# The sign step of a norm's means on GpSimd instead of VectorE

## The chip, the cores and the metric

The kernel runs on one core of a Trainium2 chip. A core has five engines that run side by side and wait for one another through semaphores: TensorE (PE in the profile, its weight loads PEld), VectorE (DVE), ScalarE (ACT), GpSimd (POOL) and SyncE (SP), which here issues the DMAs. The metric is the device time of one execution in microseconds; of several runs the median is given.

## The reference

One transformer block is computed on 2048 tokens of width 512, in bf16. Each half has a norm without weights, a modulation by rows that come from a conditioning vector, a mixer, and a gated residual.

```python
x = A_x
h = _layernorm(x, axis=-1) * (1 + ca) + sa
x = x + ga * _A_ref(h, A_wqkv, A_wo)        # 32 heads of 16, causal window of 256 keys
h = _layernorm(x, axis=-1) * (1 + cb) + sb
x = x + gb * _B_ref(h, B_w1, B_b1, B_w2, B_b2)

def _layernorm(x, axis=-1, eps=1e-05):
    m = jnp.mean(x, axis=axis, keepdims=True)
    v = jnp.var(x, axis=axis, keepdims=True)
    return (x - m) / jnp.sqrt(v + eps)
```

`_B_ref` norms its input once more and then mixes over tokens: `u = gelu(h^T w1 + b1)` with 1792 hidden features, and `y = u w2 + b2`. So there are three norms per token: n1 ahead of attention, n2 behind it, and n3 inside the token mixer.

## The kernel before

The 2048 tokens are 16 blocks of 128 (partitions are tokens). `xres[t]` holds block t of the residual stream. Four blocks make a group `tg`. The program has three stages.

1. A prologue up to about 13 us: masks, the modulation, n1 of the first four blocks, the first query and key projections.
2. The attention stage, 16 steps of 4 heads on 512 queries each (`s` = 4·tg + g8). ScalarE takes 152 exponentials of 128x1024 (L868). TensorE makes the scores for them, and between the scores does the projections, the products with V (L890), the output projection `Wo` (L606 or L610 by its shape), and the first half of the token mixer. VectorE empties PSUM, transposes, and does the statistics of the norms.
3. The tail from about 157 us: `Wo` and the norms of the last four blocks (12 to 15) run while TensorE does the second half of the first token-mixing product (matmuls out<-hb,w1b on L606), and then the second token-mixing product (L1451) with its output steps.

A norm that is laid through the class `Norm` is done for 1, 2 or 4 blocks together. It has these instructions, in this order:

- `stats`: per block a BATCH_NORM_STATS2 (L599) and a BATCH_NORM_AGGREGATE (L600) on VectorE, which leave mean and variance side by side in the tile `mv`.
- `prepare`: on VectorE `ve` = variance + epsilon (L571) and `neg` = −mean (L575). The profile calls their outputs n1ve, n1ng, n2ve, and so on by the norm.
- `rstd`: on GpSimd `r` = ve to the power −1/2 (L582) and `shift` = neg · r (L584, n2sh and so on).
- `apply`: per block one instruction r·x + shift, on ScalarE (L588), or on VectorE or GpSimd (L592).

Behind n2's apply come two row operations, a multiplication by bc_cb and an addition of bc_sb (L1273), then n3's statistics, and n3's apply writes `hb[tb]`, the operand of the first token-mixing product. The tiles of `prepare` and `rstd` come from the pool `small`, 4 buffers to a name.

Which engine does what is set per block in the table `BY`, whose entries for the last blocks are

```python
'p2.12': 'POOL', 'k2.12': 'POOL', 'm2.12': 'DVE', 'p3.12': 'ACT',
'p2.13': 'POOL', 'k2.13': 'DVE', 'm2.13': 'DVE', 'p3.13': 'POOL',
'p2.14': 'ACT', 'k2.14': 'DVE', 'm2.14': 'DVE', 'p3.14': 'POOL',
'p2.15': 'DVE', 'k2.15': 'DVE', 'm2.15': 'DVE', 'p3.15': 'DVE',
```

(p2 and p3 are the applies of n2 and n3, k2 and m2 the row operations). How many blocks share a norm is set by `JOINT`; the last four blocks have one norm each. In all `prepare` runs 20 times: 3 for n1, 8 for n2, 9 for n3. Twelve are in the attention stage and eight, one of n2 and one of n3 for each of the blocks 12 to 15, in the tail.

The order of the work is made by a small planner (`Order`): every step is a task with an engine, a cost, what it needs, and a rank; the planner plays the engines forward, and `emit` then writes the tasks in order of their planned starts. Every engine executes its own instructions in the order in which they were written. A whole `prepare` is one task (`e1.`, `e2.`, `e3.`) with the engine "DVE" and a cost of 0.13, and a whole `rstd` is one task on "POOL" (`q2.`, `q3.`, `r1.`); GpSimd tasks that were planned between the two stand between them on GpSimd.

On TensorE the second half of the first token-mixing product goes through the tokens block by block: eight matmuls on hb_12, then eight on hb_13, eight on hb_14, and six on hb_15 ahead of the next features. The first matmul of each block waits for the engine that writes that block's `hb`: for ScalarE (12), GpSimd (13 and 14) and VectorE (15).

Of the kernel before, what the change touches and what calls it, by code (L numbers as in the profile page):

```python
# [347 lines left out]
def kernel(  # L348
# [14 lines left out]
    nc = tc.nc  # L363
# [194 lines left out]
    class Norm:  # L558
# [9 lines left out]
        def prepare(self):  # L568
            n = self.n
            self.ve = small.tile([P, n], DT.float32, name=self.name + "ve")  # L570
            nc.vector.tensor_scalar(  # L571
                out=self.ve[:], in0=self.mv[:, :, 1], scalar1=EPS, scalar2=0.0, op0=ALU.add, op1=ALU.add
            )
            self.neg = small.tile([P, n], DT.float32, name=self.name + "ng")
            nc.vector.tensor_scalar(  # L575
                out=self.neg[:], in0=self.mv[:, :, 0], scalar1=-1.0, scalar2=0.0, op0=ALU.mult, op1=ALU.add
            )

# [923 lines left out]
```

## Time and profile before

| | |
|---|---|
| time of 3 runs | 243.13 us median, 242.91 to 243.34 |
| profiled execution | 242.64 us, of it a span of 240.9 us |
| PE busy | 234.5 us (97%) |
| DVE busy | 177.3 us (74%) |
| ACT busy | 162.1 us (67%) |
| POOL busy | 96.1 us (40%) |
| sign step on DVE (L575) | 20 instructions |

The span is the time between the first and the last instruction of the profiled execution. An engine's share is a mean over stages with different limits: ScalarE is full during attention and nearly idle in the tail, while GpSimd has its work in bursts. The lines "idle before" name what ended a wait. In the tables of instructions below, the first number is the start in us from the start of the span, the second the duration.

### The profile page before, as it was taken

The numbers are of one execution on the slowest core, as the hardware profiler recorded it, in microseconds if no ns is written. First come the engines' busy times: TensorE is split into PE (matmuls) and PEld (weight loads), VectorE is DVE, ScalarE is ACT, GpSimd is POOL, SyncE is SP. The second block draws the span as 40 slices with busy tenths as digits, with TensorE's granted clock in tenths as the row PEclk, the third lists the DMA queues.
The fourth block names the chain that finished last, engine by engine and source line by source line (L and its number), as shares of the span: only waits on it lengthen the run. The fifth ranks groups of instructions, "written<-read, shape, count | busy, mean of one in ns | idle before, by whom it ended". The sixth has DMA issues, their size and how long they took to land.

```text
span 240.9 us, 9884 instructions
## 1 busy us (share of the span) xinstructions
PE 234.5 (97%) x4358; PEld 118.7 (49%) x4358; DVE 177.3 (74%) x421; ACT 162.1 (67%) x188; POOL 96.1 (40%) x149
## 2 busy tenths in 40 slices
PE   7999999999999999999999999999999999999994
PEld 2545555545655554554454455454444444444443
DVE  8799998878999899999356867989964306060644
ACT  7589999999999999999999999900446400000000
POOL 5319775741655466996310113686920000000000
PEclk9999999999999999999999999999999999999999
DMA  5998714063160343210110110069999001111031
GB/s 161 303 345 245 224 32 123 21 169 68 58 181 5 74 113 91 64 35 7 33 38 14 26 38 3 3 199 393 413 405 407 18 0 46 44 44 44 24 111 44
DMA packets 26151, 28.09 MB, mean 117 GB/s; under 512 B 10488, under 2 KB 23292, under 8 KB 26108
## 3 DMA queue, kind: packets, MB, share of 16 engines
q1 hardware_dynamic: 25956, 27.33, 36.0%
q8 instruction: 34, 0.56, 1.0%
q10 hardware_dynamic: 152, 0.13, 0.2%
q14 instruction: 9, 0.07, 0.1%
HBM read 22.55 MB, written 2.10 MB: 102 GB/s over the span
## 4 chain that ended last, share of the span: by engine, by line
PE 74%; DVE 19%; POOL 2%; issue 2%; ACT 2%; DVEq 0%; ACTq 0%; POOLq 0%
PE bk L606 18%; PE pss L1451 15%; PE bk L890 7%; PE pss L606 6%; PE bk L610 6%; PE pss L847 6%; DVE stats L599 5%; PE bk L1451 5%; PE bk L624 3%; DVE x L1255 2%; DVE t L899 2%; PE pss L859 2%; PE pss L819 2%; PE pss L828 1%; DVE QR L740 1%
## 5 line engine op out<-in xcount | busy, mean ns | idle before, releaser
L868 ACT ACTIVATE et<-pss 128x1024 bf16<-128x1024 f32 x152 | 141.7, 1050 | 1.5 <-PE pss L859 1.3
L1451 PEld LDWEIGHTS <-w2r 128*128 128x128 bf16 x238 | 23.1, 98 | 25.5
L912 POOL TENSOR_TENSOR merge<-t,zr 128x512 bf16<-128x512 f32 x16 | 16.9, 1058 | 32.3 <-DVE zr L908 32.2
L1460 DVE SCALAR_TENSOR_TENSOR o<-pss,bFM,bc_gb 128x512 bf16<-128x512 f32 (+2 forms) x13 | 8.8, 705 | 27.9 <-PE pss L1451 27.9
L1451 PE MATMUL pss<-guT,w2r 128*128 128x512 bf16 (+2 forms) x130 | 28.4, 363 | 0.0
L899 DVE STREAM_TRANSPOSE t<-bk 128x512 f32<-128x512 f32 x32 | 22.6, 706 | 7.2 <-PE bk L890 7.0
L847 PE MATMUL pss<-QP,KT 32*128 32x64 bf16 (+2 forms) x672 | 24.2, 236 | 0.7 <-DVE QP L727 0.3
L606 PE MATMUL bk<-h1T,wqkv 128*128 128x512 bf16 x80 | 21.0, 381 | 0.0
L1048 POOL TENSOR_SCALAR QP<-QR,mask_par 128x512 bf16<-128x512 bf16 x22 | 15.1, 694 | 14.8 <-PE pss L859 9.7
L606 PE MATMUL bk<-hb,w1a 128*128 128x512 bf16 x82 | 20.6, 380 | 0.2 <-DVE t L899 0.2
L606 PE MATMUL pss<-hb,w1b 128*128 128x512 bf16 x80 | 20.1, 379 | 0.1
L847 PEld LDWEIGHTS <-KT 32*128 32x128 bf16 x672 | 11.2, 92 | 17.7 <-issue 15.1
L890 PE MATMUL bk<-et,V 128*32 128x256 bf16 (+2 forms) x704 | 19.0, 240 | 0.7 <-DVE t L899 0.4
L599 DVE BATCH_NORM_STATS2 stats<-x 128x6 f32<-128x512 bf16 x28 | 18.8, 673 | 0.2
L890 PEld LDWEIGHTS <-V 128*32 128x32 bf16 x704 | 15.2, 97 | 7.2 <-issue 2.7
L606 PEld LDWEIGHTS <-w1b 128*128 128x128 bf16 x112 | 10.9, 98 | 13.7 <-issue 0.5
L859 PE MATMUL pss<-mask_q,mask_k 32*128 32x256 bf16 x240 | 17.5, 268 | 0.0
L606 PE MATMUL bk<-wod,OT 128*128 128x512 bf16 x54 | 13.9, 381 | 0.0
L606 PEld LDWEIGHTS <-w1a 128*128 128x128 bf16 x90 | 7.9, 98 | 10.3 <-issue 2.5
L606 PE MATMUL bk<-wqkv,h1T 128*128 128x512 bf16 x47 | 12.8, 381 | 0.0
L1255 DVE TENSOR_TENSOR x<-bk,x 128x512 bf16<-128x512 f32 x16 | 10.8, 674 | 2.8 <-PE bk L606 2.8
L921 DVE STREAM_TRANSPOSE OT<-merge 128x512 bf16<-128x512 bf16 x16 | 11.2, 700 | 2.0 <-POOL merge L912 1.8
(145 smaller groups left out, 396.5 us busy)
## 6 DMA issues: line engine op xcount, KB each, us to landing
w2r<-in_B_w_dram SPq DMA_DIRECT2D x14, 512.0 KB, 10.6
w1a<-in_B_w_dram SPq DMA_DIRECT2D x16, 224.0 KB, 3.7
w1b<-in_B_w_dram SPq DMA_DIRECT2D x8, 448.0 KB, 6.7
wmod<-in_w_mod_dram SPq DMA_DIRECT2D x4, 512.0 KB, 6.9
x<-in_A_x_dram SPq DMA_DIRECT2D x15, 128.0 KB, 5.4
out_dram<-otile SPq DMA_DIRECT2D x15, 128.0 KB, 1.8
VL<-V SPq DMA_DIRECT2D x15, 96.0 KB, 2.3
wmod<-in_w_mod_dram SPq DMA_DIRECT2D x4, 256.0 KB, 4.3
```

The costliest lines, as they stand in the source:

```text
L599: nc.vector.bn_stats(out=stats[:], in_=src)
L606: nc.tensor.matmul(out[:], lhsT=lhsT, rhs=rhs, start=start, stop=stop, skip_group_check=True)
L610: nc.tensor.matmul(out[cols, :], lhsT=lhsT[:, cols], rhs=rhs, start=start, stop=stop, tile_position=(0, 32 * j), skip_group_check=True,)
L847: mm(pss[j // 2][:, j % 2, c0 : c0 + nq], lhsT=keys(4 * tg + kb)[rows[j], :], rhs=QP[s][rows[j], par, q0 : q0 + nq], start=n == 0, stop=False,
L859: mm(o, lhsT=mask_k[rows[j], 0:P], rhs=rhs, start=False, stop=True, tile_position=(32 * j, 0), skip_group_check=True,)
L868: nc.scalar.activation(out=et[:], in_=held.pop(("pss", u, a))[:], func=ACT.Exp, scale=SCORE_SCALE)
L890: nc.tensor.matmul(po[32 * j : 32 * j + 32, q0 : q0 + nq], lhsT=v(j), rhs=held["et", s, k, j // 2][:, j % 2, c0 : c0 + nq], start=n == 0, ...
L899: nc.vector.transpose(out=held["t2", s][:, par, :], in_=psum.pop(("po", s, par))[:])
L912: nc.gpsimd.tensor_tensor(out=m[:].rearrange("p (b a d) -> p a b d", a=2, d=DH), in0=t2v(s, 0, DH, DH), in1=held["zr", s][:].to_broadcast( ...
L1048: engine[by(f"Qp{s}.{par}", "POOL")].tensor_scalar(out=QP[s][:, par, :], in0=QR[s][:], scalar1=mask_par[:, par : par + 1], scalar2=0.0, op ...
L1255: nc.vector.tensor_tensor(out=xres[tb][:], in0=pa[:], in1=xres[tb][:], op=ALU.add)
L1451: nc.tensor.matmul(py[:, lo:hi], lhsT=w2r[:, fc, tb * P : (tb + 1) * P], rhs=guT[fc][:, lo:hi], start=fc == made[0], stop=fc == made[-1], ...
```

## The change

The instruction that makes `neg` is issued on GpSimd instead of VectorE. It reads the same means and writes the same tile with the same arithmetic; `ve` stays on VectorE.

```diff
             nc.vector.tensor_scalar(
                 out=self.ve[:], in0=self.mv[:, :, 1], scalar1=EPS, scalar2=0.0, op0=ALU.add, op1=ALU.add
             )
             self.neg = small.tile([P, n], DT.float32, name=self.name + "ng")
-            nc.vector.tensor_scalar(
+            nc.gpsimd.tensor_scalar(
                 out=self.neg[:], in0=self.mv[:, :, 0], scalar1=-1.0, scalar2=0.0, op0=ALU.mult, op1=ALU.add
             )
```

The planner's tasks, costs and ranks are not touched, so all other instructions keep their order: PE, ACT and SP have the same rows before and after, VectorE has 20 rows fewer, GpSimd 20 more.

The first place is on VectorE in the attention stage, at the second n1 norm (the number behind a name tells instances of a tile apart; h1T is the normed, modulated and transposed input of the projections, bk a PSUM bank):

```order
 L1155 TENSOR_SCALAR h1T_863<-bk1_862,modFM0_93 128x512 x2
 L571 TENSOR_SCALAR n1ve_913<-n1mv_586 128x4
-L575 TENSOR_SCALAR n1ng_915<-n1mv_586 128x4
 L1155 TENSOR_SCALAR h1T_863<-bk0_900,modFM1_94 128x512 x2
 L899 STREAM_TRANSPOSE t2_976<-bk1_919 128x512
```

The second pair of h1T instructions now follows n1ve directly.

The second place is GpSimd in the tail, from n2's last row operation of block 12 (h2_5651) to n3's shift of block 12 (n3sh_5718); h2_5688 is n2's apply of block 13:

```order
 L1273 TENSOR_TENSOR h2_5651<-h2_5651,bc_cb1_99 128x512
+L575 TENSOR_SCALAR n2ng_5670<-n2mv_5643 128x1
 L582 TENSOR_TENSOR n2r_5678<-n2ve_5668,mhalf_91 128x1
 L584 TENSOR_TENSOR n2sh_5680<-n2ng_5670,n2r_5678 128x1
 L592 TENSOR_SCALAR h2_5688<-x13_77,n2r_5678,n2sh_5680 128x512
+L575 TENSOR_SCALAR n2ng_5692<-n2mv_5673 128x1
 L582 TENSOR_TENSOR n2r_5702<-n2ve_5690,mhalf_91 128x1
 L584 TENSOR_TENSOR n2sh_5704<-n2ng_5692,n2r_5702 128x1
+L575 TENSOR_SCALAR n3ng_5711<-n3mv_5695 128x1
 L582 TENSOR_TENSOR n3r_5716<-n3ve_5709,mhalf_91 128x1
 L584 TENSOR_TENSOR n3sh_5718<-n3ng_5711,n3r_5716 128x1
```

Three sign steps (n2 of blocks 13 and 14, n3 of block 12) now stand on GpSimd ahead of the shift that n3's apply of block 12 needs.

The third place follows directly on GpSimd, and ends at n3's apply of block 14 (hb_14); hb_13 is that of block 13:

```order
+L575 TENSOR_SCALAR n2ng_5724<-n2mv_5655 128x1
 L582 TENSOR_TENSOR n2r_5733<-n2ve_5722,mhalf_91 128x1
 L584 TENSOR_TENSOR n2sh_5735<-n2ng_5724,n2r_5733 128x1
+L575 TENSOR_SCALAR n3ng_5744<-n3mv_5727 128x1
 L582 TENSOR_TENSOR n3r_5747<-n3ve_5742,mhalf_91 128x1
 L584 TENSOR_TENSOR n3sh_5749<-n3ng_5744,n3r_5747 128x1
 L592 TENSOR_SCALAR hb_13_123<-h2_5688,n3r_5747,n3sh_5749 128x512
+L575 TENSOR_SCALAR n3ng_5767<-n3mv_5755 128x1
 L582 TENSOR_TENSOR n3r_5771<-n3ve_5765,mhalf_91 128x1
 L584 TENSOR_TENSOR n3sh_5773<-n3ng_5767,n3r_5771 128x1
 L592 TENSOR_SCALAR hb_14_124<-h2_5720,n3r_5771,n3sh_5773 128x512
```

Two more sign steps stand ahead of hb_13, and a sixth ahead of hb_14. No instruction of GpSimd other than the sign steps is added or moved past another.

## The prediction

> **What bounds the kernel now.** I read the page's head and groups first, to see which engine is full in which stage.
>
> ```profile
> span 240.9 us, 9884 instructions
> PE 234.5 (97%) x4358; PEld 118.7 (49%) x4358; DVE 177.3 (74%) x421; ACT 162.1 (67%) x188; POOL 96.1 (40%) x149
> PE 74%; DVE 19%; POOL 2%; issue 2%; ACT 2%; DVEq 0%; ACTq 0%; POOLq 0%
> L868 ACT ACTIVATE et<-pss 128x1024 bf16<-128x1024 f32 x152 | 141.7, 1050 | 1.5 <-PE pss L859 1.3
> ```
>
> The third line is the chain that ended last: GpSimd has 2% of it, so a GpSimd that is busy 40% looks like free room. The fourth says what limits attention: 152 exponentials keep ScalarE busy 141.7 us, with 1.5 us of idle time ahead of them in all. Work on other engines shortens that stage by no more than this idle time. The tail is read in windows (columns after the stretch: PE, PEld, DVE, ACT, POOL busy with their instructions, clock, DMA share, GB/s), and the length of a matmul in the chain.
>
> ```profile
> 160.00:180.00 20.00, 19.94 (x92) 8.79 (x91) 17.17 (x53) 4.66 (x6) 12.95 (x26) 1.00 1.01 393
> 180.00:200.00 20.00, 20.00 (x95) 9.00 (x94) 5.16 (x9) 7.07 (x12) 0.00 (x0) 1.00 0.36 143
> 182.45 6.91 PE pss L606 x32
> ```
>
> 32 matmuls in 6.91 us are 0.216 us each, and 92 of them fill 19.9 of the 20 us from 160. TensorE has no slack there, and a stall of it moves the end one for one. At the same time GpSimd works 12.95 of 20 us, so the place to look at is who feeds TensorE in that window.
>
> **What is removed from VectorE.** 20 sign steps leave it:
>
> ```profile
> L575 DVE TENSOR_SCALAR n3ng<-n3mv x9: 143/153/161, 87.3 to 175.3; 128x2 f32<-128x2 f32 x4, 128x1 f32<-128x1 f32 x4, 128x4 f32<-128x4 f32 x1
> L575 DVE TENSOR_SCALAR n2ng<-n2mv x8: 142/152/598, 63.7 to 170.2; 128x1 f32<-128x1 f32 x4, 128x4 f32<-128x4 f32 x2, 128x2 f32<-128x2 f32 x2
> L575 DVE TENSOR_SCALAR n1ng<-n1mv x3: 159/165/600, 18.7 to 36.2; 128x4 f32<-128x4 f32 x3
> ```
>
> Two of them took about 0.6 us (the third number is the maximum), the others 0.14 to 0.17. They overlap with their neighbours, so one is worth the spacing of starts. One of the long ones lies in front of a visible wait; these are rows of VectorE, GpSimd, TensorE and ScalarE at that place:
>
> ```profile
> 27.43 0.98 DVE L1155 TENSOR_SCALAR h1T<-bk,modFM 128x512 bf16<-128x512 bf16 x2
> 28.34 0.16 DVE L571 TENSOR_SCALAR n1ve<-n1mv 128x4 f32<-128x4 f32 x1
> 28.41 0.60 DVE L575 TENSOR_SCALAR n1ng<-n1mv 128x4 f32<-128x4 f32 x1
> 28.91 0.98 DVE L1155 TENSOR_SCALAR h1T<-bk,modFM 128x512 bf16<-128x512 bf16 x2
> 27.62 1.36 POOL L1048 TENSOR_SCALAR QP<-QR,mask_par 128x512 bf16<-128x512 bf16 x2 [0.46 <-DVE QR L740]
> 29.95 1.05 PE L610 MATMUL bk<-wqkv,h1T 128*32 128x512 bf16 x16 [0.35 <-DVE h1T L1155]
> 32.03 8.36 ACT L868 ACTIVATE et<-pss 128x1024 bf16<-128x1024 f32 x9 [0.40 <-PE pss L859]
> 153.69 2.89 ACT L868 ACTIVATE et<-pss 128x1024 bf16<-128x1024 f32 x3
> ```
>
> n1ng ended at 29.01, just as GpSimd's QP ended at 28.98: it stood behind that instruction. The pair of h1T ahead of it, which reads PSUM, took its 0.98 us beside the same QP, so the next pair needn't wait for it. With n1ng gone, that pair starts at about 28.41 instead of 28.91, TensorE's wait of 0.35 us goes, and ScalarE's 0.40 us goes with it up to 0.35. From there ScalarE is continuous up to its last exponential, which ends at 153.69 + 2.89 = 156.58, so that one can come 0.35 us earlier if the feeders keep pace. I take −0.35 us: the other waits on the way are on engines of the same chain and shift with it. Bounds: 0 if a later wait swallows it, −0.40 since this idle stretch is the one behind 20 us that ScalarE has.
>
> The Trainium skill, "SBUF — State Buffer", section "Who interferes with whom", says that a VectorE instruction in a two-port mode and a GpSimd instruction exclude each other for a whole instruction. The row of n1ng agrees (0.60 us, ended with QP). The same rule speaks against the change, since GpSimd's sign steps can then stand behind VectorE; that is a rival below.
>
> The other eleven sign steps of the attention stage cost nothing on GpSimd where it has a gap; where it has none its applies start later by one step, under exponentials that are queued back to back. If that cover were gone, a step would cost its spacing, worked out next.
>
> **What is added to GpSimd.** The trace has no sign step there. Nearest rows: a small TENSOR_SCALAR (L634), with an independent instruction behind it; one with a dependent instruction behind it (L553, L555); and two memsets, which read nothing.
>
> ```profile
> 0.94 0.10 POOL L389 MEMSET mhalf<- 128x4 f32 x1
> 0.98 0.10 POOL L393 MEMSET plus_mod<- 128x2 f32 x1
> 3.78 0.26 POOL L634 TENSOR_SCALAR sig<-sig 128x4 f32<-128x4 f32 x1
> 3.99 0.23 POOL L487 TENSOR_SCALAR_AFFINE_SELECT seed<-seed 16x64 bf16<-16x64 bf16 x1
> 4.92 0.24 POOL L553 TENSOR_SCALAR r_ve<-mv 128x2 f32<-128x2 f32 x1 [0.71 <-DVE mv L646]
> 5.25 0.74 POOL L555 TENSOR_TENSOR r<-r_ve,mhalf 128x2 f32<-128x2 f32 x1
> ```
>
> Start to start these are 0.21, 0.33 and 0.04 us. The sign step is the first kind: the power behind it reads ve, not neg. So p = 0.21 us, between 0.04 and 0.33. By its duration (0.26) it would be more. The Trainium skill, "Perfetto Trace Analysis", section "GPSIMD Engine Instruction", advises spacing over reported duration; the rows with 0.26 long and 0.21 apart agree, and by the duration the sum below would be 0.3 us higher.
>
> Now the tail. GpSimd's rows from block 12's row operation on:
>
> ```profile
> 164.53 0.55 POOL L582 TENSOR_TENSOR n2r<-n2ve,mhalf 128x1 f32<-128x1 f32 x1 [1.78 <-DVE n2ng L575]
> 166.31 1.15 POOL L1273 TENSOR_TENSOR h<-h,bc_cb 128x512 bf16<-128x512 bf16 x1
> 167.43 0.56 POOL L582 TENSOR_TENSOR n2r<-n2ve,mhalf 128x1 f32<-128x1 f32 x1
> 168.35 0.83 POOL L592 TENSOR_SCALAR h<-x,n2r,n2sh 128x512 bf16<-128x512 bf16 x1
> 169.15 0.54 POOL L582 TENSOR_TENSOR n2r<-n2ve,mhalf 128x1 f32<-128x1 f32 x1
> 169.94 0.72 POOL L582 TENSOR_TENSOR n3r<-n3ve,mhalf 128x1 f32<-128x1 f32 x1
> 170.73 0.19 POOL L584 TENSOR_TENSOR n3sh<-n3ng,n3r 128x1 f32<-128x1 f32 x1
> 170.88 0.54 POOL L582 TENSOR_TENSOR n2r<-n2ve,mhalf 128x1 f32<-128x1 f32 x1
> 172.74 0.77 POOL L592 TENSOR_SCALAR hb<-h,n3r,n3sh 128x512 bf16<-128x512 bf16 x1
> 174.56 0.77 POOL L592 TENSOR_SCALAR hb<-h,n3r,n3sh 128x512 bf16<-128x512 bf16 x1
> 175.46 0.55 POOL L582 TENSOR_TENSOR n3r<-n3ve,mhalf 128x1 f32<-128x1 f32 x1
> ```
>
> Only the first row stands behind an idle stretch (1.78 us). There the sign step of block 12 falls into the gap, and the power starts as soon as ve is there, 0.07 us earlier by the spacing of n1ve and n1ng above. From 166.31 to 175.33 GpSimd is back to back, so every sign step there pushes all that follows by p. On the way to hb_12 there are three (n2 of 13 and 14, n3 of 12), to hb_13 five (with n2 of 15, n3 of 13), to hb_14 six (with n3 of 14). Who waits for them, on ScalarE, TensorE, TensorE in the chain, and VectorE:
>
> ```profile
> 170.96 0.81 ACT L588 ACTIVATE hb<-h,n3sh,n3r 128x512 bf16<-128x512 bf16 x1 [0.15 <-POOL n3sh L584]
> 171.17 1.25 PE L606 MATMUL pss<-hb,w1b 128*128 128x512 bf16 x4
> 172.25 0.38 PE L606 MATMUL bk<-hb,w1b 128*128 128x512 bf16 x1
> 171.82 0.59 PE pss L606 x2
> 176.31 0.41 DVE L592 TENSOR_SCALAR hb<-h,n3r,n3sh 128x512 bf16<-128x512 bf16 x1 [0.88 <-POOL n3sh L584]
> ```
>
> hb_12 is ready at 171.77 and TensorE starts on it at 171.82: the four matmuls from 171.17 take 1.25 us instead of 0.38 + 3 × 0.216 = 1.03, so it already waits 0.2 us. Each block has eight matmuls, 1.73 us. TensorE reaches hb_13 at 173.55, which is ready at 172.74 + 0.77 = 173.51; it reaches hb_14 at 175.28, ready at 175.33. All three arrive just in time, so there is no slack at any. hb_15 is ready at 176.72 and needed at about 177.1: 0.4 us of slack.
>
> With p = 0.21: hb_12 comes 3 × 0.21 − 0.07 = 0.56 us later, hb_13 5 × 0.21 − 0.07 = 0.98, hb_14 6 × 0.21 − 0.07 = 1.19. TensorE's stalls add up to the largest, 1.19. hb_15 is late by a seventh step, 1.40 at most, under 1.19 + 0.4. VectorE's apply of block 15 waits for GpSimd too, but its result feeds only hb_15. Behind hb_15 there is no GpSimd work, and TensorE, full in the second window, cannot catch up. The eight sign steps that leave VectorE in the tail bring nothing but the 0.07: VectorE waits for GpSimd there.
>
> **Sum.** +1.19 in the tail (bounds 6 × 0.04 − 0.07 = +0.17 and 6 × 0.33 − 0.07 = +1.91), −0.35 in attention (0 to −0.40): +0.84 us. The profiled execution took 242.64 us, so 243.48 for one like it. The median of the runs, 243.13, is 0.49 above it, and I put the sum on the median: 244.0 us.
>
> **Rivals.** *The early gain is lost, the tail stays.* ScalarE's 0.40 us comes back as a wait somewhere in the 125 us behind it, at a GpSimd step that is late by p. For it: GpSimd's n1r there starts p later. Against it: ScalarE had only 1.5 us of idle time in all. Time: 243.13 + 1.19 = 244.3.
>
> *The sign step hides in the issue of its neighbours, so the kernel is not slower.* The price of a step decides. The two memsets, 0.04 us apart, speak for it; the TENSOR_SCALAR at 0.21 and the shift at 170.73, which with two inputs of one column still holds the next row 0.15 us off, speak against it. With 0.04: +0.17 − 0.35 = −0.18, 242.95. Below p = 0.07 the sum is a gain, below p = 0.15 it is under the half microsecond that a measurement of this kernel can tell from no change (0.2%).
>
> *The lock.* Equal powers of one column take 0.54 to 0.56 us as n2r and 0.72 as n3r at 169.94, while VectorE runs two-input row operations. If every sign step of the tail lost such 0.17 us too, the tail would be 1.19 + 6 × 0.17 = 2.21, and the time 243.13 + 2.21 − 0.35 = 245.0. Against it: only some of the steps meet such an instruction. By the rule of "SBUF — State Buffer" in the Trainium skill quoted above, section "Who interferes with whom", two SBUF inputs suffice for this; n3r agrees.
>
> That the change does not do what it says is no rival: only its engine differs.
>
> **Chances.** Forecast 0.47, lost gain 0.23, hidden step 0.20, lock 0.10. The first is slower by more than 0.2% nearly always (244.0 is 0.35% up), the second and the fourth always, the third is no change (0.14) or faster (0.06). So slower 0.74, no change 0.19, faster 0.07. The range goes from the hidden step, 242.9, to most of the lock, 244.8; the forecast's own range is 243.7 to 244.4.
>
> **What would show it.** In the trace after: GpSimd's sign steps in the tail 0.2 us ahead of the next power; TensorE waiting some 0.6 us longer at hb_12, 0.4 at hb_13 and 0.2 at hb_14 while the rows up to 166 keep their places against each other; at the second n1 norm h1T right behind n1ve, TensorE's wait of 0.35 us gone, and the last exponential, which ends at 156.6 now, at about 156.2. The prediction is wrong if the sign steps are spaced under 0.15 us, if the last exponential ends later than now, or if TensorE's stall comes at hb_15 instead, which would mean that VectorE and not GpSimd is late there.

## The result, and the profile after

The changed kernel took 245.06 us in the median of 4 runs (244.24 to 245.48), the kernel before 243.08 beside it (242.91 to 243.34): a ratio of 1.0078, interval 1.0061 to 1.0095. That is slower, as forecast, but above the range. On another chip the same kernel took 244.37 (243.77 to 245.02) beside 243.19, a ratio of 1.0046 (1.0027 to 1.0065). The profiled execution of the first measurement took 244.24 us, the fastest of its four, with a span of 242.3; against the profiled execution of before (242.64) it is 1.60 us longer, 1.4 of them in the span. The reading below goes by these two traces, and by the others as they come.

The page's head, the chain that ended last, and the exponentials of the changed kernel:

```profile
span 242.3 us, 9866 instructions
PE 234.7 (97%) x4358; PEld 118.6 (49%) x4358; DVE 176.2 (73%) x401; ACT 162.1 (67%) x188; POOL 99.4 (41%) x169
PE 85%; POOL 5%; DVE 4%; ACT 3%; issue 2%; DMA 1%; ACTq 0%
L868 ACT ACTIVATE et<-pss 128x1024 bf16<-128x1024 f32 x152 | 141.8, 1050 | 1.7 <-PE pss L859 1.5
```

GpSimd's share of the chain went from 2% to 5%, and ScalarE's idle time ahead of the exponentials went up by 0.2 us instead of down. Twenty instructions changed engine; VectorE is 1.1 us less busy and the kernel is longer. The same kernel in windows (columns after the stretch: PE, PEld, DVE, ACT, POOL busy, clock, DMA share, GB/s):

```profile
160.00:180.00 20.00, 18.99 (x87) 8.20 (x85) 16.44 (x42) 3.27 (x4) 14.74 (x35) 1.00 1.01 391
180.00:200.00 20.00, 20.00 (x94) 9.11 (x93) 6.56 (x11) 8.46 (x14) 0.00 (x0) 1.00 0.37 150
```

Between 160 and 180 us TensorE was busy 19.94 us before and 18.99 now, and GpSimd 14.74 instead of 12.95. So TensorE does stall in the tail. The timeline of the changed kernel shows where (GpSimd's sign steps and the applies they push, then what TensorE and VectorE do with them):

```profile
166.56 1.15 POOL L1273 TENSOR_TENSOR h<-h,bc_cb 128x512 bf16<-128x512 bf16 x1
167.69 0.19 POOL L575 TENSOR_SCALAR n2ng<-n2mv 128x1 f32<-128x1 f32 x1
167.84 0.55 POOL L582 TENSOR_TENSOR n2r<-n2ve,mhalf 128x1 f32<-128x1 f32 x1
171.73 0.46 POOL L575 TENSOR_SCALAR n2ng<-n2mv 128x1 f32<-128x1 f32 x1
172.16 0.53 POOL L582 TENSOR_TENSOR n2r<-n2ve,mhalf 128x1 f32<-128x1 f32 x1
174.00 0.77 POOL L592 TENSOR_SCALAR hb<-h,n3r,n3sh 128x512 bf16<-128x512 bf16 x1
174.73 0.36 POOL L575 TENSOR_SCALAR n3ng<-n3mv 128x1 f32<-128x1 f32 x1
175.04 0.53 POOL L582 TENSOR_TENSOR n3r<-n3ve,mhalf 128x1 f32<-128x1 f32 x1
175.96 0.77 POOL L592 TENSOR_SCALAR hb<-h,n3r,n3sh 128x512 bf16<-128x512 bf16 x1
171.72 0.42 DVE L1273 TENSOR_TENSOR h<-h,bc_cb 128x512 bf16<-128x512 bf16 x1
174.34 0.70 DVE L1273 TENSOR_TENSOR h<-h,bc_cb 128x512 bf16<-128x512 bf16 x1
172.67 0.59 PE L606 MATMUL pss<-hb,w1b 128*128 128x512 bf16 x2 [0.68 <-ACT hb L588]
174.81 0.38 PE L606 MATMUL bk<-hb,w1b 128*128 128x512 bf16 x1 [0.26 <-POOL hb L592]
178.28 0.59 PE L606 MATMUL bk<-hb,w1b 128*128 128x512 bf16 x2
```

GpSimd's row operation at 166.56 stood at 166.31 before, so everything here is 0.25 us late to begin with. On top of that, TensorE's first product of block 12 comes 172.67 − 171.82 − 0.25 = 0.60 us later, hb_13 is ready 174.77 − 173.51 − 0.25 = 1.01 later, hb_14 176.73 − 175.33 − 0.25 = 1.15. The first pair of products on hb_15 stands at 178.28; it stood at 176.89, by this row of before:

```profile
176.89 0.59 PE L606 MATMUL bk<-hb,w1b 128*128 128x512 bf16 x2
```

That is 178.28 − 176.89 − 0.25 = 1.14 later, as late as hb_14 made it. From there on TensorE is full again.

A sign step takes 0.19 us, and the next power starts 0.15 us behind its start (167.69, 167.84). Two of the six are longer, at 171.73 and 174.73, both beside a two-input row multiplication on VectorE (the two L1273 rows of DVE). The six spacings are 4 × 0.15 + 0.43 + 0.31 = 1.34 us. The whole stretch, from the first of these steps (before: the power at 167.43) to hb_14's apply, grew from 7.13 to 8.27 us, by 1.14: the other instructions got 0.20 us shorter in sum. Three powers (n3r) that met such a row operation before took 0.72, 0.72 and 0.70 us and now take 0.53 to 0.55, while one power and one shift grew by 0.20 and 0.19. So 6 × 0.15 = 0.90 us of the 1.14 are the steps themselves, and 0.24 are such meetings.

The early place, in the changed kernel's timeline:

```profile
28.33 0.16 DVE L571 TENSOR_SCALAR n1ve<-n1mv 128x4 f32<-128x4 f32 x1
28.40 0.99 DVE L1155 TENSOR_SCALAR h1T<-bk,modFM 128x512 bf16<-128x512 bf16 x2
28.94 0.20 POOL L575 TENSOR_SCALAR n1ng<-n1mv 128x4 f32<-128x4 f32 x1
29.52 1.05 PE L610 MATMUL bk<-wqkv,h1T 128*32 128x512 bf16 x16
30.40 0.47 PE L890 MATMUL bk<-et,V 128*32 128x256 bf16 x11
31.23 0.26 PE L890 MATMUL bk<-et,V 128*32 128x192 bf16 x4 [0.35 <-issue]
32.22 8.36 ACT L868 ACTIVATE et<-pss 128x1024 bf16<-128x1024 f32 x9 [0.59 <-PE pss L859]
153.95 2.89 ACT L868 ACTIVATE et<-pss 128x1024 bf16<-128x1024 f32 x3
```

h1T stands right behind n1ve, and TensorE starts on it at 29.52 instead of 29.95. Then, behind the eleventh of 16 products with V (L890), TensorE stops for 0.35 us, put down to "issue", and ScalarE waits 0.59 us where it waited 0.40. The last exponential ends at 156.84, 0.26 us later than before.

What holds TensorE there? The values of step 2 of attention are copied from V to a second layout (VL and VU), and this copy lands at about that time, behind the 512 KB load of wod. SyncE's queue in the changed kernel, and the time from issue to landing in the DMA view:

```profile
22.61 1.67 SPq L1006 DMA_DIRECT2D wod<-in_A_wo_dram  x1
25.49 0.60 SPq L1077 DMA_DIRECT2D VL<-V  x1
VL<-V SPq DMA_DIRECT2D x1, 96.0 KB, 5.6
```

and in the kernel before, with the copy of step 3 as the last row:

```profile
25.35 0.60 SPq L1077 DMA_DIRECT2D VL<-V  x1
VL<-V SPq DMA_DIRECT2D x1, 96.0 KB, 5.4
31.54 0.60 SPq L1077 DMA_DIRECT2D VL<-V  x1
```

Before, the copy landed at 25.35 + 5.4 = 30.75; in the changed kernel it lands at 31.09, and TensorE goes on at 31.23. From these times I took the copy for the cause, and the experiments with wod were laid out to test it. They show that wod's load matters. The copy, however, is not what TensorE waits for; the traces that rule it out stand behind the table further down.

### The profile page after: what moved, and what is told of

It reads as the page before. It is cut to its first block, busy times and chain, and to the rows that moved or that the text cites. A ratio compares the mean times of both kernels' runs of the same rounds, so it can differ in the third digit from the quotient of the medians.

```text
span 242.3 us, 9866 instructions
## 1 busy us (share of the span) xinstructions
PE 234.7 (97%) x4358; PEld 118.6 (49%) x4358; DVE 176.2 (73%) x401; ACT 162.1 (67%) x188; POOL 99.4 (41%) x169
## 4 chain that ended last, share of the span: by engine, by line
PE 85%; POOL 5%; DVE 4%; ACT 3%; issue 2%; DMA 1%; ACTq 0%
PE bk L606 24%; PE pss L1451 15%; PE bk L890 8%; PE pss L847 8%; PE bk L610 7%; PE bk L1451 5%; PE pss L606 5%; ACT et L868 3%; PE pss L859 3%; PE pss L819 2%; PE bk L624 2%; PE pss L828 2%; POOL n2r L582 1%; PE bk L1142 1%; PE pss L610 1%
## 5 line engine op out<-in xcount | busy, mean ns | idle before, releaser
L890 PE MATMUL bk<-et,V 128*32 128x256 bf16 (+2 forms) x704 | 19.2, 240 | 1.0 <-DVE t L899 0.4
L890 PEld LDWEIGHTS <-V 128*32 128x32 bf16 x704 | 15.2, 97 | 7.8 <-issue 3.4
```

Of the source, the lines that this page charges most:

```text
L890: nc.tensor.matmul(po[32 * j : 32 * j + 32, q0 : q0 + nq], lhsT=v(j), rhs=held["et", s, k, j // 2][:, j % 2, c0 : c0 + nq], start=n == 0, ...
```

## The experiments

**The same kernel again, each half alone, and a form without the sign step.** These four ran on one chip.

> The changed kernel once more, for a second trace of it. Theory T (the price is six GpSimd steps in front of hb_14 in the tail, about 1.15 us as in the first trace, and anything above it comes from small shifts upstream): 1.2 to 2.0 us slower than before, TensorE's stalls at hb_12, hb_13 and hb_14 adding up to 1.0 to 1.4 us, and the last exponential 0 to 0.8 us later than before. Rival A (the rest of the loss lies in the attention stage): the same total, but with the last exponential over 0.8 us later.

Measured: 244.37 us, ratio 1.0046 (1.0027 to 1.0065), +1.18 on the medians.

One half alone, the eight norms of one block:

```diff
-            nc.gpsimd.tensor_scalar(
+            (nc.gpsimd if n == 1 else nc.vector).tensor_scalar(
                 out=self.neg[:], in0=self.mv[:, :, 0], scalar1=-1.0, ...
```

> The sign step on GpSimd only for the eight one-block norms of the tail; the other twelve stay on VectorE. Theory T: 1.1 to 1.3 us slower than before, the attention stage as before, so the last exponential at 156.6 give or take 0.1. Rival A: the tail's 1.15 us alone, and less than two thirds of the changed kernel's loss. If the tail itself varies from run to run (GpSimd's small steps meeting VectorE's two-input adds or not), the times of this kernel spread by 0.5 us or more while before's spread by 0.2.

Measured: 244.33 us (244.14 to 244.62), ratio 1.0046 (1.0031 to 1.0061): all of the slowdown.

The other half, the twelve norms of several blocks, with `n > 1` in that line:

> The sign step on GpSimd only for the twelve norms of the attention stage; the eight of the tail stay on VectorE. Theory T: between 0.3 us faster and 0.3 us slower than before. Rival A: 0.5 to 1.0 us slower, with the last exponential later by as much. The prediction's early gain, if it existed, would show as 0.35 us faster.

Measured: 242.95 us, ratio 0.9995 (0.9975 to 1.0016). No slowdown, and no gain of 0.35 either. (Its profiled execution took 246.35 us and is left out of what follows.) So the tail's half carries the whole price, and the other half is worth nothing as it stands.

The last one drops sign step and shift from all norms but the two that ScalarE applies, and applies (x − mean) · r:

```diff
-                    out=out, in0=src, scalar1=self.r[:, i : i + 1], scalar2=self.shift[:, i : i + 1],
-                    op0=ALU.mult, op1=ALU.add,
+                    out=out, in0=src, scalar1=self.mv[:, i, 0:1], scalar2=self.r[:, i : i + 1],
+                    op0=ALU.subtract, op1=ALU.mult,
```

> No sign step and no shift at all where VectorE or GpSimd apply a norm: they compute (x - mean) * r in one instruction, as the prologue does; only the two norms that ScalarE applies (n2 of block 14, n3 of block 12) keep both, on VectorE and GpSimd as before. So GpSimd loses its shift in front of hb_13 and hb_14 instead of gaining a sign step. Theory T: TensorE's waits at hb_12 to hb_14, 0.3 us in before, go, and the kernel is 0.2 to 0.4 us faster than before, plus up to 0.35 us if VectorE's relief in attention reaches the end. Rival A: the relief of VectorE disturbs attention, so no gain or a loss.

Measured: 262.68 us, ratio 1.0793 (1.0760 to 1.0826). The lines of this edit (the apply is L596 there), first and last number of the three being the shortest and the longest in ns:

```profile
L596 POOL TENSOR_SCALAR hb<-h,n3mv,n3r x12: 2071/2077/2193, 94.5 to 193.0; 128x512 bf16<-128x512 bf16 x12
L596 DVE TENSOR_SCALAR h<-x,n2mv,n2r x8: 404/407/414, 73.6 to 189.7; 128x512 bf16<-128x512 bf16 x8
L872 ACT ACTIVATE et<-pss 128x1024 bf16<-128x1024 f32 x152 | 142.1, 1043 | 14.5 <-PE pss L863 12.7
```

and the same apply in the kernel before:

```profile
L592 POOL TENSOR_SCALAR hb<-h,n3r,n3sh x12: 766/772/802, 88.8 to 174.6; 128x512 bf16<-128x512 bf16 x12
```

On GpSimd the apply went from 0.77 to 2.08 us when (multiply, add) became (subtract, multiply), with the mean and r as its scalars in place of r and the shift; on VectorE it stayed at 0.41. GpSimd has 27 of them, some 35 us more work, and ScalarE waits 14.5 us ahead of its exponentials. The run tells nothing of the sign step: the side effect is many times as large, and I had not reckoned with it.

**Is it the V copy?** The 512 KB load of wod stands ahead of step 2's copies in SyncE's queue and isn't needed until later. Three kernels issue it behind them, and the order of everything else stays. What stood behind wod then starts earlier, the V copies and all other transfers alike, so these runs test wod's load and not the copy alone:

```diff
-        later("wo", wod[:], wo_v, 512, 12)
+        add("L.wo", "SP", 512 / 345.0, lambda: None, rank=12, after=1.0, lag=2.8)
 ...
             dma.dma_start(out=VU ...)
+            if s == 2:
+                dma.dma_start(out=wod[:], in_=wo_v)
```

> The kernel before, with one transfer moved: the 512 KB load of wod is issued behind the V copies of step 2 instead of ahead of them. Theory (the gain of the change's attention part is eaten by the V copy, which lands behind wod): the V copy of step 2 lands about 1.5 us earlier than 30.8 us, and nothing else in this kernel waits for it at present, so ScalarE's idle time ahead of the exponential at 32 us stays at 0.40 us, made by h1T; the time is that of the kernel before, 243.1, within 0.3 us. Rival (the copy already sets this gap here too, by its scatter): the median falls by 0.2 to 0.4 us.

> The change, with wod's load behind the V copies of step 2. Theory: with the V copy early, the attention part keeps what the prediction gave it: ScalarE's idle ahead of the exponential at 32 us falls from 0.59 to under 0.2 us and only the tail's price stays; against the kernel before +0.8 (243.9), against the change as it is -0.5 to -1.1. Rival (the gain is lost elsewhere than at the copy): the idle time comes back at a later exponential, and the time stays at 244.4 to 245.1.

> Only the 12 many-block norms' sign steps on GpSimd (the tail keeps VectorE), with wod's load behind the V copies of step 2. Theory: 0.35 us faster than the kernel before, 242.75, and as much faster than the kernel before with wod late. Rival (h1T's earlier end is worth nothing whatever the copy does): the same as the kernel before with wod late.

Measured, on one chip beside 243.08 for the kernel before: 242.79 us, ratio 0.9990 (0.9968 to 1.0011); 243.81, 1.0031 (1.0009 to 1.0053); 242.21, 0.9955 (0.9937 to 0.9972). The moved load by itself is worth nothing that can be told; its median, 0.29 below, fits its rival as well, and the idle time below decides. With it, the attention half of the change is worth 242.79 − 242.21 = 0.58 on the medians, where 0.35 was expected; the two intervals touch. Rows of the third kernel, SyncE, DMA, TensorE and ScalarE:

```profile
24.82 0.60 SPq L1077 DMA_DIRECT2D VL<-V  x1
26.17 0.59 SPq L1085 DMA_DIRECT2D wod<-in_A_wo_dram  x1
VL<-V SPq DMA_DIRECT2D x1, 96.0 KB, 4.8
29.35 1.05 PE L610 MATMUL bk<-wqkv,h1T 128*32 128x512 bf16 x16
25.66 15.05 ACT L868 ACTIVATE et<-pss 128x1024 bf16<-128x1024 f32 x16
```

The copy lands at 29.62, TensorE goes through the products without a stop, and ScalarE runs 16 exponentials in a row through the place where it stood idle. In the first of the three the idle time is what h1T made it:

```profile
32.17 2.85 ACT L868 ACTIVATE et<-pss 128x1024 bf16<-128x1024 f32 x3 [0.40 <-PE pss L859]
```

**What does a step cost in the tail?** The change, with a second sign step behind the first in the eight one-block norms; nothing reads its output.

```diff
+            if n == 1:
+                twin = small.tile([P, n], DT.float32, name=self.name + "ng2")
+                nc.gpsimd.tensor_scalar(
+                    out=twin[:], in0=self.mv[:, :, 0], scalar1=-1.0, scalar2=0.0, op0=ALU.mult, op1=ALU.add
+                )
```

> The change, with a second sign step on GpSimd behind the first in each of the eight one-block norms; its output is not read. It measures the price of a small GpSimd instruction in the chain. Theory (each step costs its spacing, 0.15 us alone and more beside a two-input row addition, mean 0.2, six of them on the path): +0.9 to +1.3 us on the change, 245.3 to 246.3 by its two measurements of 244.4 and 245.1; the first double product of the last block comes 2.0 to 2.4 us later than in the kernel before, from the start of the tail. Rival (the price is not the spacing but the crossing from one engine to the other, paid once): within 0.3 us of the change.

Measured: 245.67 us (245.56 to 245.99), ratio 1.0096 (1.0062 to 1.0130), within the theory's times. In its timeline:

```profile
166.70 1.15 POOL L1278 TENSOR_TENSOR h<-h,bc_cb 128x512 bf16<-128x512 bf16 x1
167.82 0.19 POOL L575 TENSOR_SCALAR n2ng<-n2mv 128x1 f32<-128x1 f32 x1
167.97 0.19 POOL L580 TENSOR_SCALAR n2ng<-n2mv 128x1 f32<-128x1 f32 x1
168.12 0.55 POOL L587 TENSOR_TENSOR n2r<-n2ve,mhalf 128x1 f32<-128x1 f32 x1
179.67 0.59 PE L611 MATMUL bk<-hb,w1b 128*128 128x512 bf16 x2
```

Again 0.15 us from step to step. The first product pair on hb_15 comes 179.67 − 166.70 = 12.97 us after the row operation: 11.72 with one sign step, 10.58 with none on GpSimd. The second set of six cost 1.25, the first 1.14. The price goes by the number of steps.

**Does another engine cost as much?** ScalarE is nearly idle in the tail (4.66 of the 20 us from 160 were busy before) and computes neither the means nor the power. Its sign step is `nc.scalar.activation(out=self.neg[:], in_=self.mv[:, :, 0], func=ACT.Identity, scale=-1.0)` for `n == 1`; in the first kernel all else is as before, the second has the other twelve on GpSimd and wod late. With them ran the attention half with wod late and as it was.

> The kernel before, with the sign steps of the eight one-block norms on ScalarE, which neither takes the mean nor the power. Theory (the tail's price is the sign step's place on GpSimd's own chain, between the mean and the power; moving it off VectorE is in itself a small gain): the sign step runs beside the power, which takes 0.55 us, and VectorE loses 0.06 to 0.07 us per norm, six of them on the path: 0 to -0.4 us, 242.7 to 243.1; the first double product of the last block comes 10.2 to 10.6 us after the GpSimd row addition at 166.31 us (10.58 before, 11.72 with the change). The table load that stands behind the last sign step on ScalarE begins at 175.6 instead of 171.8 us and still ends ahead of the first gate at 178.25. Rival (the price is a crossing between engines and comes with any other engine): about +1.2 us, 244.3.

> The 12 many-block norms' sign steps on GpSimd, the eight one-block ones on ScalarE, and wod's load behind the V copies of step 2. Theory: both gains, at 32 us and in the tail, 0 to 0.4 us faster than the kernel without the ScalarE part (242.2): 241.8 to 242.2. Rival: as that kernel with +1.2, 243.4.

> The 12 many-block norms' sign steps on GpSimd, wod's load behind the V copies, once more on this chip beside the next: 242.2 again (the kernel before less 0.6 to 0.9).

> The 12 many-block norms' sign steps on GpSimd, wod's load where it was. Theory (the V copy eats the gain): ScalarE's idle ahead of the exponential at 32 us is 0.5 to 0.9 us and TensorE's wait for h1T is gone; the time is the kernel before's within 0.3 us and 0.4 to 0.8 above the same kernel with wod late. Rival (the copy doesn't matter and the earlier difference was of the chip): as fast as that kernel.

Measured beside 242.67 us for the kernel before: 242.86, ratio 1.0012 (0.9996 to 1.0028); 242.80, 0.9992 (0.9978 to 1.0006); 242.31, 0.9979 (0.9962 to 0.9995); 242.54, 1.0001 (0.9983 to 1.0019). The tail with ScalarE's steps:

```profile
167.68 1.16 POOL L1276 TENSOR_TENSOR h<-h,bc_cb 128x512 bf16<-128x512 bf16 x1
176.59 0.15 DVE L571 TENSOR_SCALAR n3ve<-n3mv 128x1 f32<-128x1 f32 x1
176.59 0.20 ACT L576 ACTIVATE n3ng<-n3mv 128x1 f32<-128x1 f32 x1 [1.87 <-DVE n3mv L603]
176.83 0.54 POOL L585 TENSOR_TENSOR n3r<-n3ve,mhalf 128x1 f32<-128x1 f32 x1
178.25 0.59 PE L609 MATMUL bk<-hb,w1b 128*128 128x512 bf16 x2
```

and in the kernel before:

```profile
175.22 0.15 DVE L571 TENSOR_SCALAR n3ve<-n3mv 128x1 f32<-128x1 f32 x1
```

178.25 − 167.68 = 10.57 us, as before (10.58). So the price is not a crossing between engines that any other engine would bring: it is GpSimd's, which does the power too. ScalarE brought no gain either: the second kernel, forecast at 241.8 to 242.2, took 242.80, against 242.31 for the same without ScalarE's steps. The power starts 0.24 us behind ve whether or not VectorE has a sign step in between (176.59 to 176.83 here, 175.22 to 175.46 before). VectorE's sign step was covered by the crossing from ve to the power, so nothing could be saved by taking it away.

The traces together. The last two columns are the time from the start of the exponential row at 25 to 27 us to the end of the last exponential, and from the start of GpSimd's row operation at 166 to 168 us to the first product pair on hb_15. "q8 ends" is the end of a transfer that is explained below the table, from its start and duration in the trace:

| kernel | n1's sign step | wod | V copy lands | q8 ends | ScalarE idle near 32 us | exponentials | tail |
|---|---|---|---|---|---|---|---|
| before | VectorE | ahead | 30.75 | 29.42 | 0.40 | 130.72 | 10.58 |
| one-block half alone | VectorE | ahead | 31.30 | 29.98 | 0.87 | 131.21 | 11.88 |
| before, wod late | VectorE | behind | 28.27 | 27.87 | 0.40 | 130.73 | w1b late |
| before, tail on ScalarE | VectorE | ahead | 32.08 | 30.38 | 0.47 | 131.48 | 10.57 |
| change | GpSimd | ahead | 31.09 | 29.77 | 0.59 | 131.00 | 11.72 |
| change, again | GpSimd | ahead | 31.69 | 30.33 | 0.87 | 131.27 | 11.75 |
| many-block half, again | GpSimd | ahead | 30.77 | 29.47 | 0.68 | 131.04 | w1b late |
| second step in the tail | GpSimd | ahead | 31.06 | 29.78 | 0.96 | 131.33 | 12.97 |
| change, wod late | GpSimd | behind | 30.75 | 29.28 | 0 | 130.30 | 11.75 |
| many-block half, wod late | GpSimd | behind | 29.62 | 28.27 | 0 | 130.39 | 10.59 |
| the same, again | GpSimd | behind | 29.48 | 27.94 | 0 | 130.27 | 10.64 |
| the same, tail on ScalarE | GpSimd | behind | 29.05 | 27.53 | 0 | 130.32 | 10.76 |

With wod ahead, all four kernels with n1's sign step on GpSimd keep an idle stretch, and their exponentials take 0.28 to 0.61 us longer than before; with wod behind, all four have none and take 0.33 to 0.45 us less. Two kernels with attention as before lost time as well, 0.49 and 0.76 us. The one-block half alone stops at the same place, for 0.21 us, without any early h1T. With the tail on ScalarE, most of the loss is a second idle stretch, 0.48 us ahead of the exponential at 35.17, behind VectorE, which waited 0.67 us for a load of x. "w1b late" stands where TensorE waited ahead of this stretch for the load of w1b and the whole tail came later; in the many-block half, again:

```profile
164.32 0.60 PE L606 MATMUL pss<-hb,w1b 128*128 128x512 bf16 x2 [1.15 <-DMA w1b<-in_B_w_dram]
```

That execution took 244.06 us where the median was 242.54. The medians show the gain of the many-block half less cleanly than the traces: 0.58 on one chip, on the other 242.54 − 242.31 = 0.23, where 0.4 to 0.8 was expected and the intervals overlap.

**Which transfer is it?** Not the V copy. VL and VU have two buffers, used by turns. The products at 31 us are the second half of step 1 (by the kernel a step has 8 heads, four in each half) and read the buffer that the copy of step 2 does not write. SyncE issues the copy of step 3, which overwrites the buffer of step 1, at 31.54 in the kernel before, just behind these products; the next products, those of step 2, come at 36.14. With the tail on ScalarE, TensorE even loads weights from VL at 31.77, ahead of that copy's landing at 32.08:

```profile
31.77 0.17 PEld L893 LDWEIGHTS <-VL 128*32 128x32 bf16 x10
```

And in all five traces of the table that stop (the change twice, each half, the second step), TensorE stops at the same weight load, the 483rd of the program: the twelfth of 16 from V, and none from VL. Its product reads the same block of V and the same tile of exponentials as the eleventh, which did not wait, so data are not what was missing.

A fixed place in the program points to the arrival of TensorE's own instructions. One DMA queue is named for them. This is its line on the changed kernel's page (packets, MB, share), and in the DMA view from 28.6 to 29.8 us:

```profile
q8 instruction: 34, 0.56, 1.0%
q8 instruction: 1, 0.02, 5.6%
```

34 transfers of 16 KB are 557 KB, some 64 bytes for each of TensorE's 2 × 4358 matmuls and weight loads, while no other engine has over 401 instructions on that page; so I estimate that q8 brings TensorE's instructions. The one transfer of that window ends at 29.77, and TensorE goes on at the 483rd weight load at 31.22, 1.45 us later. In the other four traces that stop it is 1.56 to 1.62 us. With the tail on ScalarE it is 1.37, with a gap of 0.08 us. In the kernel before it is 1.52 and there is no gap: TensorE came just in time, with little or no slack. With wod behind, the transfer ends 1.74 us or more ahead of that weight load, and nothing stops. This fits every trace of the table. But no run moves the instruction transfer alone: that wod's load ahead of it costs the gain is tested, and that it does so through this transfer is read from the traces.

## Why the prediction was right and wrong

- **Direction: right.** Slower, ratios 1.0078 and 1.0046. The size was not: 1.98 us on the first medians, where 0.84 was forecast.
- **Tail +1.19: right, 1.14 to 1.17 measured** in the three traces that have all of the change (11.72, and 11.75 twice, against 10.58), and 1.30 in the one-block half alone. The cumulative stalls 0.56, 0.98, 1.19 came out as 0.60, 1.01, 1.15, all without slack as read from the kernel before, and hb_15 added nothing. The doubled step confirms the count of six: 1.25 more.
- **p = 0.21: right as a mean, for another reason.** A step alone takes 0.15 us, not 0.21. Two of six meet a two-input row operation of VectorE and take 0.43 and 0.31. So the rival of the lock was true in part: two steps lost 0.28 and 0.16 us beside such an operation, and the other instructions got back 0.20 of it. The Trainium skill, "SBUF — State Buffer", section "Who interferes with whom", states that a VectorE instruction with two SBUF inputs contends with a GpSimd instruction that reads SBUF; these two rows agree (0.46 and 0.36 us long, 0.19 else).
- **−0.07 at block 12: wrong, 0.** The power starts 0.23 us behind ve both before (164.30 to 164.53) and after (164.56 to 164.79). VectorE's spacing was not on that path, by the same cover that the run with ScalarE showed.
- **Attention −0.35: the step that failed.** Its first link held: h1T moved up 0.51 us, TensorE's wait at the projections was gone, and TensorE started 0.43 earlier. What failed is "ScalarE's 0.40 us goes with it up to 0.35 ... if the feeders keep pace". TensorE did not keep pace: it stopped for 0.35 us at the 483rd weight load, a place where the kernel before has no stop and, by the traces, little or no slack. ScalarE waited 0.59 us instead of 0.40, and the exponentials got 0.28 us longer instead of 0.35 shorter. The last one ended later than before, which the prediction had named as a sign that it is wrong. The bounds of 0 to −0.40 left this out: they took the wait behind the removed one to be no later than before. With wod's load moved, the step holds, and its size was right: the exponentials take 0.33 to 0.45 us less, and the last ends at 25.66 + 130.39 = 156.05, where 156.2 was foretold. That the stop is the arrival of instructions, delayed by wod, is argued above and not tested by itself.
- **The rival "the early gain is lost, the tail stays", 244.3,** is what happened, though some 1 us behind the removed wait, at TensorE, and not at a GpSimd step in the 125 us behind it. The second chip's 244.4 is at it.
- **The forecast 244.0, range to 244.8.** Between the two profiled executions the sum +0.84 met +1.60: tail +1.14, exponentials +0.28, and the rest, 0.2 us, outside the span. The first median of 245.06 is 0.8 above its own profiled execution, where that of the kernel before is 0.4 above its own, and it lies above the range. The other three executions have no trace. The stop near 31 us (idle times of 0.59 to 0.96 us in four traces with the early h1T) and waits for w1b are of a size to do it, but that they did is not shown, and this part stays open.

The version that came out fastest is the many-block half on GpSimd, the one-block norms left on VectorE, and wod's load behind step 2's copies: ratios 0.9955 and 0.9979, both intervals under 1.

## What to carry to other kernels

Moving a small instruction to a less busy engine is priced by the chain that it joins there: eight steps on the engine that also computes the power cost 1.14 us, the same steps on ScalarE nothing, and on VectorE they had been covered by a 0.24 us crossing. Where a wait is removed, look up what the waiting engine meets next, the arrival of its own instructions included: a stop put down to "issue" at the same instruction in several traces names no data. A gain that doesn't come may only stand behind a large load in the queue, and moving that load brought it out here. And check which buffer an instruction reads before a transfer that lands at the right time is taken for the cause.

## What was unexpected of the hardware

- A GpSimd apply of 128x512 in bf16 with two per-partition scalars took 0.77 us as (multiply, add) and 2.07 to 2.08 us as (subtract, multiply), in the median of each norm; VectorE took 0.41 us for n2's applies in both.
- GpSimd's sign step of one column has a duration of 0.19 us and a spacing of 0.15; beside two-input row operations of VectorE it took 0.36 and 0.46.
- A 96 KB copy issued at 25 us, behind 512 KB loads, took 5.4 to 5.9 us to land, and 3.8 to 5.4 with one such load moved behind it.
- TensorE stopped for 0.21 to 0.78 us at one and the same weight load in five traces, 1.45 to 1.62 us behind the end of a 16 KB transfer on the instruction queue. With a 512 KB load moved back, that transfer ended at 27.5 to 29.3 us instead of 29.4 to 30.4, and the stop was gone.
